# Routing of 128-token tiles to experts: row products queued behind the choice of the tile ahead, rank products at other steps, the last tile's split in a second buffer

## The chip, the cores and the metric

The kernel runs on one core of a Trainium2 chip. The metric is device time in microseconds of one launch, the median of the runs shown. Engines by the names of the profile: PE (TensorE), DVE (VectorE), ACT (ScalarE), POOL (GpSimd), SP (SyncE, which issues most DMAs). A time is better the smaller it is.

## What is computed

The reference, cut to what matters: causal attention of 2 x 12 heads (448 positions, head size 64), a dense layer with squared relu, then a layer of eight experts where each token goes to the one expert of its largest logit.

```python
scores = where(mask, -1e9, q @ k.T / sqrt(64))          # causal
x = softmax(scores) @ v                                  # -> 896 tokens x 768
h = maximum(x @ w_in, 0); x = h * h @ w_out              # 768 -> 2048 -> 768
xn = x / (norm(x) + 1e-6); en = emb / (norm(emb) + 1e-6) # 8 experts
logits = xn @ en.T / tau; idx = argmax(logits, axis=1)
gate = softmax(logits)[idx]
for e in range(8):
    m = idx == e
    out[m] = gate[m] * (maximum(x[m] @ w1[e], 0) @ w2[e]) # 768 -> 1024 -> 768
```

## The kernel before

**Precision.** Operands are split into a high half that ACT rounds (line 65) and a low half that DVE takes as the rest (line 72); three products, high by high, high by low, low by high, make one full product. So each weight piece and each block of activations costs ACT one pass and DVE one.

**Stages.** PE's instructions stand in the order in which they are written. Attention fills PE until about 180 us, the product with `w_in` until about 250. Then `b_tiles` forms y = h²·w_out for seven tiles of 128 tokens (line 639): tiles 0 and 1 together until 257.7, then tile 2, 3, 4, 5 and 6 one by one until 352.9. A tile has 16 column steps f of three pairs of matmuls (`wo<f>h`, `wo<f>l`, `wo<f>h` again). At step ends 3, 7, 11 ACT and DVE split the next part of h² into `hs`; that reuses a buffer which PE must have read. Then comes the first expert, run early with tokens known by then (`mm1`, lines 948 to 950, 352.9 to 373.3: eight blocks ft of six kc-steps of three matmuls; `mm2`, line 1036, to 392), and then all other experts, to the end.

**Routing a tile.** `route_tile(t)` is a generator. Hooks advance it by one `yield` when PE's written order comes to a given step: `CFG["rs"]` says for each tile of `b_tiles` at which step f which tile's routing goes on; `CFG["ft0"]`, `CFG["ft1"]` and `CFG["late"]` do that in the early expert, by pairs (ft, kc).
- Tiles 0 to 3 (`CFG["dve"]`): ACT squares the rows (`sq`, line 657), DVE forms eight row products with the experts' rows (`sv`, line 661; each is followed by a read of its sum). `choose` then does three Newton steps for the norm (lines 577 to 590), scales (705 to 708), takes maxima (710, 711), marks the expert (`c`, 716 and 717; the code's `c8`) and writes the one-hot `OH` (718), while ACT takes the exponentials (`ex`, 713). After a `yield` PE forms the rank products `rk` from `tri` and `OH` and from `ones` and the running sum `OHs` (721, 722); DVE and POOL finish gate and rank.
- Tiles 4 to 6: PE turns the rows (`yt`, 671), ACT and DVE split them into `yhl` (683, 72), PE forms the logits (`lgt`, 690), DVE copies them (`lgs`, 692), PE turns them back (`lg`, 696), DVE sums the two halves (`l`, 698), and then comes `choose`.

The last tile is routed during `mm1` of the early expert. `tables` follows it: `cnt` on PE (1161), `n` on DVE (1165), `z` and more, the ranks, a chain of small steps on POOL to `lane`, the one-hot `ol` on POOL (760), `rv` on DVE (753), and the table product `tabp` on PE (766), which gives the lists of tokens to all other experts. `ps_r`, tag `lg`, is one bank that `lgt`, `lg`, `rk`, `cnt` and `tabp` share in turn. `late` issues the high and low halves `mh`, `ml` of the last four weight pieces of the early expert.

**What sets the order elsewhere.** ACT's and DVE's instructions stand in the order of the scheduler: it goes by priority (`urgent` raises it) and by what is ready by its own estimate. `tc.issue_after(x)` keeps an instruction from being issued before x. An engine carries out its queue strictly in order, so an instruction that waits holds up all behind it.

Of the kernel before, what the change touches and what calls it, by code (L numbers as in the profile page):

```python
# [25 lines left out]
KC = DM // P  # L26
# [6 lines left out]
def f32(ap):  # L33
    return ap.bitcast(F32)


CFG = dict(
    first=1, hp=3000, xe=[1, 7, 8, 10, 12], turn=5, xfd=[3, 4, 5, 6], xfj=[1, 2, 3, 4],
    joint=1, mhi="A", rt6=[1, 4, 7, 9, 15], dve=(0, 1, 2, 3), neng=(),
    rs={2: [(1, 0), (2, 1)], 3: [(2, 2), (5, 0), (12, 1)], 4: [(1, 3), (7, 2)],  # L40
        5: [(2, 3), (2, 4), (3, 4), (4, 4), (5, 4), (7, 4)], 6: [(f, 5) for f in (1, 4, 7, 9, 15)]},
    rd={2: [], 3: [0, 1], 4: [2], 5: [3, 4], 6: [5]},
woh="A", h2h="A", h2l="V", et=[8, 8, 12],
    turn2=[1, 3], ft0=[(0, 3), (1, 3), (2, 3), (3, 3), (4, 3), (4, 5)], ft1=[3], ft2=[3, 5, 6, 7], late=[(2, 5), (4, 5)], ew=[2, 4, 10, 10, 10, 12], stop=0, mlo="V", xh="A", h2="A",
    wh="G", wil="G", wol="GV", warm=8, nsa=6, nwi=3, nwb=3, wo0=4, hs0=[4, 5, 8, 9], conv0=17, convs=2, pin=1,
    qsb=2, pb=2, ptb=2, qkraw=3, vraw=2, vb=2, ss=4, pts=2, pvs=2, pas=4, wsp=1,
    man=21,
# [6 lines left out]
def build(tc, qkd, vd, w_in, w_out, emb, tau, wm, cst, out, dbg_y=None):  # L54
    nc = tc.nc
    V, A, G, T, DMA = nc.vector, nc.scalar, nc.gpsimd, nc.tensor, nc.sync

    ENG = {"A": A, "V": V, "G": G, "S": DMA}
# [12 lines left out]
    def lo_of(eng, lo, x, hi):  # L71
        return eng.tensor_tensor(out=lo, in0=x, in1=hi, op=ALU.subtract)  # L72
# [19 lines left out]
    cs, at = constants()  # L92
# [13 lines left out]
    spool = tc.alloc_tile_pool(name="stage", bufs=2)  # L106
# [29 lines left out]
    last = {}  # L136
# [354 lines left out]
    for p in (ps_v, ps_t, ps_s):  # L491
# [4 lines left out]
    h2 = [h2a_pool.tile([P, NF, GT], F32, tag="h2", name="h2_0"),  # L496
          h2b_pool.tile([P, NF, GT], F32, tag="h2", name="h2_1")]
# [57 lines left out]
    bpool = tc.alloc_tile_pool(name="phb", bufs=1, reuse_waits="tile")  # L555
# [37 lines left out]
    es = rpool.tile([E, 1], F32, name="es")  # L593
# [8 lines left out]
    rows = []  # L602
# [8 lines left out]
    ent = rpool.tile([P, KC, 2 * E], F32R, name="ent")  # L611
# [39 lines left out]
    def route_tile(t, y):  # L651
        p0 = t * P
        DMA.dma_start(out=ydram[p0:p0 + P, :], in_=y)
        if t in CFG["dve"]:
            ss = rpool.tile([P, 1], F32, tag="ss", bufs=2, name="ss")
            sq = spool.tile([P, DM], BF16, tag="relu", name="sq")
            A.activation(sq, y, AF.Square, accum_out=ss)
            l = rpool.tile([P, E], F32, tag="l", bufs=2, name="l")
            for x in range(E):
                sv = spool.tile([P, DM], BF16, tag="relu", name="sv")  # L660
                V.tensor_tensor_reduce(out=sv, in0=y, in1=rows[x], scale=1.0, scalar=0.0, op0=ALU.mult, op1=ALU.add,
                                       accum_out=l[:, x:x + 1])
            yield from choose(t, ss, l)
            return
        lgt = ps_r.tile([2 * E, 2 * P], F32, tag="lg", name="lgt")
        ytt = []
        for c in range(2):
            yt = ps_h.tile([P, 512], F32, tag="h", name="yt")[:, :384].rearrange("p (a b) -> p a b", b=P)
            for j in range(3):
                kc = 3 * c + j  # L670
                T.transpose(yt[:, j], y[:, kc * P:(kc + 1) * P], ident)
            ytt.append(yt)
        ss = rpool.tile([P, 1], F32, tag="ss", bufs=2, name="ss")

# [24 lines left out]
        yield from choose(t, ss, l)
# [140 lines left out]

    NXR = (NF) * GT // (2 * DM)

    def pieces(s, res):

        for i2 in range(8):
            if i2 == 0 or (i2 == CFG["first"] and s[4] is not None):
                ereg = nc.sync.value_load((s[3] if i2 == 0 else s[4])[0:1, :], min_val=0, max_val=E - 1)
            r = state["raw"] % (NXR + 2)
            state["raw"] += 1
            if r < NXR:  # L850
                raw = mo["xraw"][:, r]
            else:
                raw = spool.tile([P, 2 * DM], F32, tag="raw", name="mraw")
            DMA.dma_start(out=raw, in_=wm[bass.ds(ereg, 1), :, 2 * i2:2 * i2 + 2, :].rearrange("o p a c -> (o p) (a c)"))
            for j in range(2):
                k = 2 * i2 + j
                pool, sl = slots[woslot[k]]
                hi = pool.tile([P, DM], F32R, tag=f"s{sl}h", name="mh")
                lo = pool.tile([P, DM], F32R, tag=f"s{sl}l", name="ml")
                x = raw[:, j * DM:(j + 1) * DM]  # L860
                copy_on(ENG[CFG["mhi"][k % len(CFG["mhi"])]], hi, x)
                lo_of(ENG[CFG["mlo"][k % len(CFG["mlo"])]], lo, x, f32(hi))
                res.append((hi, lo))
                yield

# [258 lines left out]
    for t in range(2, NTI):  # L1124
# [10 lines left out]
        if t == NTI - 1:  # L1135
# [4 lines left out]
            ew, ewl = slot_w(eslot)  # L1140
# [11 lines left out]
    y = ys[NTI - 1]  # L1152
# [283 lines left out]
```

## Time and profile before

| | |
|---|---|
| median of 3 runs | 548.42 us (547.64 to 549.15) |
| profiled execution, its own time | 548.6 us |
| its span | 546.9 us (1.7 outside it) |
| granted clock of PE, mean | 0.99 |
| PE busy | 529.6 us, 97% |
| DVE, ACT, POOL busy | 415.7, 287.6, 199.4 us |
| tile 2 of `b_tiles`, 257.70 to 274.90 | 17.20 us, PEclk 1.00 |
| tile 3, 274.90 to 296.12 | 21.22 us, PEclk 0.92 |
| tile 4, 296.12 to 312.90 | 16.78 us, PEclk 1.00 |
| early expert, 352.90 to 392.00 | 39.10 us, PE busy 37.88 |
| from 392.00 to the end | 154.90 us, PE busy 146.27 |

How to read it: the span is cut at the places where PE goes from one stage to the next. PE is busy nearly throughout; a stage of the same matmuls that lasts longer than its neighbour, or that has a granted clock under 1.00, holds a wait or its consequence. Busy time of the other engines matters only where PE waits for them. The rows on which the prediction rests have a section of their own below.

### The profile page before, as it was taken

To read this page: it belongs to the slowest core of one execution; us is meant where nothing else is said; L and a number is where in the kernel's file an instruction comes from. 1 tells how busy PE (TensorE), PEld (TensorE's weight loads), DVE (VectorE), ACT (ScalarE), POOL (GpSimd) and SP (SyncE) were. 2 spreads that over 40 slices of the span, in tenths; PEclk is the share of its full clock that TensorE was granted. 3 is DMA by queue.
4 is the path that set the end of the run, shared out by engine and by line. 5 is a ranking of instruction groups with operands and counts; after the bars stand their busy time and mean duration, and the time that the engine had idled before them with its cause. 6 is when DMAs were issued, how large, how long until landed. Compare 5 with 4: busy or idle time off the path is not lost.

```text
span 546.9 us, 9615 instructions
## 1 busy us (share of the span) xinstructions
PE 529.6 (97%) x3373; PEld 499.5 (91%) x3374; DVE 415.7 (76%) x976; ACT 287.6 (53%) x635; POOL 199.4 (36%) x273
## 2 busy tenths in 40 slices
PE   8999999999999999999989999999999999999993
PEld 5899999889999999999979989989999999999992
DVE  7888899756877968697997775886196998883641
ACT  7889887315335243434223226641386887863751
POOL 7898899916544642231010001015202302400010
PEclk9899999999999999999989999999999999999998
DMA  5667673331555555368000009402978889885310
GB/s 181 175 154 172 145 228 105 116 116 58 174 165 181 173 174 173 119 200 288 33 29 30 0 31 385 186 8 90 311 253 263 281 261 367 283 274 165 118 52 6
DMA packets 28473, 89.22 MB, mean 163 GB/s; under 512 B 2926, under 2 KB 12270, under 8 KB 28416
## 3 DMA queue, kind: packets, MB, share of 16 engines
q1 hardware_dynamic: 26880, 82.23, 47.3%
q0 software_dynamic: 1536, 6.29, 3.1%
q8 instruction: 28, 0.46, 0.3%
q14 instruction: 29, 0.24, 0.1%
HBM read 78.39 MB, written 6.32 MB: 155 GB/s over the span
## 4 chain that ended last, share of the span: by engine, by line
PE 91%; DVE 6%; ACT 1%; issue 1%; POOL 0%; POOLq 0%; DVEq 0%; ACTq 0%
PE yps L639 20%; PE ops L1036 11%; PE pa L347 7%; PE pa L349 7%; PE pa L348 7%; PE pv L323 6%; PE s L261 5%; PE pt L305 4%; PE hps L930 3%; PE ops L962 3%; PE ops L967 3%; PE hps L948 2%; PE hps L950 2%; PE hps L949 2%; PE hps L962 2%; PE hps L967 2%
## 5 line engine op out<-in xcount | busy, mean ns | idle before, releaser
L72 DVE TENSOR_TENSOR ml<-xraw,mh 128x768 fp32r<-128x768 f32 x64 | 59.5, 954 | 9.8 <-ACT mh L65 9.4
L65 ACT ACTIVATE mh<-xraw 128x768 fp32r<-128x768 f32 x64 | 52.1, 843 | 7.2 <-PE ops L962 5.8
L1036 PE MATMUL ops<-mh,act 128*128 128x384 f32 x224 | 53.5, 341 | 0.0
L323 PE MATMUL pv<-pt,v 128*128 128x448 f32 (+7 forms) x288 | 47.1, 296 | 0.6 <-ACT pt L65 0.6
L261 PE MATMUL s<-kh,q 128*128 128x128 f32 (+6 forms) x168 | 45.5, 317 | 0.7 <-ACT p L274 0.7
L274 ACT ACTIVATE p<-s,mn 128x192 f32<-128x192 f32 (+6 forms) x84 | 39.7, 476 | 11.9 <-DVE mn L271 5.2
L287 POOL TENSOR_SCALAR p<-p,rs 128x192 f32<-128x192 f32 (+6 forms) x84 | 44.1, 545 | 3.2 <-DVE rs L283 2.9
L130 DVE SCALAR_TENSOR_TENSOR w<-raw,w 128x768 int32<-128x768 int32 x32 | 42.5, 1330 | 0.7
L323 PEld LDWEIGHTS pv<-pt,v 128*128 128x128 f32 (+1 forms) x288 | 38.4, 163 | 2.7 <-ACT pt L65 1.2
L1036 PEld LDWEIGHTS ops<-mh,act 128*128 128x128 f32 x224 | 39.2, 188 | 0.8
L126 DVE TENSOR_SCALAR w<-raw 128x768 int32<-128x768 int32 x32 | 25.2, 786 | 18.5 <-POOL wi3l L72 7.2
L1062 POOL DMA_INDIRECT out<-osb,fsi x10 | 10.3, 1028 | 78.2 <-ACT osb L1057 48.8
L72 DVE TENSOR_TENSOR ml<-mraw,mh 128x768 fp32r<-128x768 f32 x32 | 30.1, 955 | 11.3 <-ACT mh L65 10.9
L729 POOL CAST gh<-g 128x1 fp32r<-128x1 f32 x7 | 1.4, 193 | 98.7 <-DVE g L727 40.1
L128 DVE SCALAR_TENSOR_TENSOR w<-raw,w 128x768 int32<-128x768 int32 x32 | 35.9, 1123 | 0.7
L271 DVE CUSTOM_DVE_ANT_0 s<-s,maskf 128x192 f32<-128x192 f32 (+6 forms) x77 | 31.8, 430 | 5.4 <-PE s L261 5.3
L353 ACT ACTIVATE relu<-pa 128x448 f32<-128x448 f32 x32 | 17.0, 538 | 34.9 <-PE pa L349 34.9
L72 DVE TENSOR_TENSOR pt<-pt 128x512 fp32r<-128x512 f32 x48 | 32.3, 682 | 3.2 <-ACT pt L65 3.1
L72 DVE TENSOR_TENSOR hs<-h,hs 128x512 fp32r<-128x512 f32 (+1 forms) x32 | 21.7, 689 | 16.7 <-ACT hs L65 16.4
L65 ACT ACTIVATE hs<-h 128x512 fp32r<-128x512 f32 (+1 forms) x32 | 17.8, 573 | 30.8 <-PE yps L639 27.6
L261 PEld LDWEIGHTS s<-kh,q 128*128 128x128 f32 x168 | 31.5, 203 | 2.4 <-ACT p L274 1.4
L65 ACT ACTIVATE pt<-pt 128x512 fp32r<-128x512 f32 x48 | 28.2, 600 | 6.1 <-PE pt L305 6.1
(471 smaller groups left out, 1683.1 us busy)
## 6 DMA issues: line engine op xcount, KB each, us to landing
xraw<-in_wm SPq DMA_DIRECT2D x32, 768.0 KB, 7.1
raw<-in_w_in SPq DMA_DIRECT2D x16, 768.0 KB, 4.2
raw<-in_w_out SPq DMA_DIRECT2D x16, 768.0 KB, 4.2
mraw<-in_wm SPq DMA_DIRECT2D x16, 768.0 KB, 5.0
qk<-in_qkd SPq DMA_DIRECT2D x11, 448.0 KB, 4.7
q<-qs SPq DMA_DIRECT2D x20, 224.0 KB, 3.8
v<-in_vd SPq DMA_DIRECT2D x12, 256.0 KB, 4.7
eb<-edram SPq DMA_DIRECT2D x8, 384.0 KB, 3.8
```

What stands on the lines that cost most here:

```text
L65: return A.activation(out, in_, AF.Copy, scale=scale)
L72: return eng.tensor_tensor(out=lo, in0=x, in1=hi, op=ALU.subtract)
L130: V.scalar_tensor_tensor(out=w[:, x], in0=raw[:, x, 0], scalar=29, in1=w[:, x], op0=ALU.logical_shift_right, op1=ALU.bitwise_or)
L261: T.matmul(ss, d["q2"][:, c, :, :, x].rearrange("p a b -> p (a b)"), d[y][:, :n], start=i_ == 0, stop=i_ == 2 and not first)
L274: last["exp", units.index(u), c] = A.activation(d["p"][c][:, :n], ss, AF.Exp, bias=mn, scale=1.0 if first else -1.0, accum_out=d["sm"][:, ...
L287: last["norm"] = G.tensor_scalar(out=p, in0=p, scalar1=rs[:, COL[c]:COL[c] + 1], scalar2=1.0, op0=ALU.mult, op1=ALU.mult)
L323: T.matmul(d["pv"][:, j * P:S] if h else d["pv"][0:D, j * P:S], d[x][:, j, 1:3].rearrange("p a b -> p (a b)") if h else d[x][:, j, 0], pt[ ...
L347: T.matmul(ps, wh[:, c], xhi[:, kc, gs], start=(kc == 0), stop=False)
L348: T.matmul(ps, wh[:, c], xlo[:, kc, gs], start=False, stop=False)
L349: T.matmul(ps, wl[:, c], xhi[:, kc, gs], start=False, stop=(kc == KC - 1))
L639: T.matmul(ps[t][c][:, :384], x, w[:, c * 384:(c + 1) * 384], start=(f == 0 and w is wh and x is hi), stop=(f == NF - 1 and x is lo))
L1036: T.matmul(ps[c], x, ww[:, col[c]], start=(fc == 0 and x is hh and ww is wh), stop=(fc == 7 and x is hl))
```

## The change

For tiles 0 to 3 the row products are now written inside `issue_after` on the `OH` of the tile ahead (from tile 1 on). Three rank products stand at earlier steps: `rk(0)` at step 2 of tile 3 (was 5), `rk(1)` at step 10 (was 12), `rk(2)` at step 5 of tile 4 (was 7). In the last tile the second `yhl` has a buffer of its own (tag `ysb`, two buffers) and both halves are split one behind the other, with the six `lgt` products in a row at (1,2); `lg` moves from (3,3) to (2,0), `rk` from (4,3) to (3,3), `cnt` from (4,5) to (4,1). The last four weight pieces are issued at (2,1) and (4,2) instead of (2,5) and (4,5), and their low halves on DVE are held behind `OH` of the last tile (first two) and behind `n` (last two).

```diff
-    rs={2: [(1, 0), (2, 1)], 3: [(2, 2), (5, 0), (12, 1)], 4: [(1, 3), (7, 2)],
+    rs={2: [(1, 0), (2, 1)], 3: [(2, 2), (2, 0), (10, 1)], 4: [(1, 3), (5, 2)],
...
-    turn2=[1, 3], ft0=[(0, 3), (1, 3), (2, 3), (3, 3), (4, 3), (4, 5)], ft1=[3], ft2=[3, 5, 6, 7], late=[(2, 5), (4, 5)], ew=[2, 4, 10, 10, 10, 12], stop=0, mlo="V", xh="A", h2="A",
+    turn2=[1, 3], ft0=[(0, 3), (1, 2), (2, 0), (3, 3), (4, 1)], ft1=[3], ft2=[3, 5, 6, 7], late=[(2, 1), (4, 2)], ew=[2, 4, 10, 10, 10, 12], stop=0, xh="A", h2="A",
...
-            for x in range(E):
+            with tc.issue_after(last["oh"].ins) if t else nullcontext():
+                for x in range(E):
...
+        due = []
         for c in range(2):
-            yhl = bpool.tile([P, 3, 2, P], F32R, tag="yhl", name="yhl")
+            again = t == NTI - 1 and c == 1
+            yhl = bpool.tile([P, 3, 2, P], F32R, name="yhl", **(dict(tag="ysb", bufs=2) if again else dict(tag="yhl")))
             last["yh"] = A.copy(yhl[:, :, 0], ytt[c])
             last["yl"] = lo_of(V, yhl[:, :, 1], ytt[c], f32(yhl[:, :, 0]))
+            due.append((c, yhl))
             if t == NTI - 1 and c == 0:
                 square()
+                continue
             yield
-            for j in range(3):
-                kc = 3 * c + j
+            for d, x in due:
+                for j in range(3):
+                    kc = 3 * d + j
...
-                lo_of(ENG[CFG["mlo"][k % len(CFG["mlo"])]], lo, x, f32(hi))
+                with ExitStack() as es:
+                    for at in pin:
+                        es.enter_context(tc.issue_after(at))
+                    lo_of(V, lo, x, f32(hi))
...
     def late():
-        while True:
+        for at in ("oh", "n"):
+            pin.append(last[at].ins)
...
+            pin.clear()
```

DVE around `OH` of tile 0. Before, the products that stand between the steps of the choice are tile 2's; all eight of tile 1 stand further ahead, between the Newton steps (`ISA` is a row product or the read of its sum):

```order
L717 TENSOR_REDUCE m<-c_3156 128x1
L589 TENSOR_TENSOR ynr<-ynr,ynt 128x1
L661 ISA sv,l<-ysb,eb 128x768
L661 ISA l 128x1
L661 ISA sv,l<-ysb,eb 128x768
L661 ISA l 128x1
L726 TENSOR_SCALAR g<-m 128x1
L718 TENSOR_SCALAR OH<-ct,m 128x8
```

And the same place in the changed kernel:

```order
L724 TENSOR_REDUCE m<-c_3156 128x1
L589 TENSOR_TENSOR ynr<-ynr,ynt 128x1
L733 TENSOR_SCALAR g<-m 128x1
L725 TENSOR_SCALAR OH<-ct,m 128x8
L662 ISA sv,l<-ysb,eb 128x768
L662 ISA l 128x1
L662 ISA sv,l<-ysb,eb 128x768
L662 ISA l 128x1
```

Tile 1's products moved from ahead of `OH` of tile 0 to behind it, and tile 2's from there to behind `OH` of tile 1.

PE in tile 3, at step 2, as a piece of the difference (the rank products of tile 0, with their weight loads):

```order
 L639 MATMUL yps<-wo1l,hs 128x384 x2
 L639 MATMUL yps<-wo1h,hs 128x384 x2
+L728 LDWEIGHTS tri
+L728 MATMUL rk<-OH,tri 128x8
+L729 LDWEIGHTS ones
+L729 MATMUL rk<-OHs,ones 128x8
 L639 MATMUL yps<-wo2h,hs 128x384 x2
 L639 MATMUL yps<-wo2l,hs 128x384 x2
```

They moved here from three steps later, between `wo4h` and `wo5h`.

DVE in the last tile, from the end of the logits to the choice, before (`ml` are low halves of weight pieces, `act` the early expert's own results):

```order
L692 COPY lgs<-lgt 16x256
L72 TENSOR_TENSOR ml<-xraw,mh 128x768 x2
L954 SCALAR_TENSOR_TENSOR act<-hps,act 128x2x128 x2
L698 TENSOR_REDUCE l<-lg 128x8
L954 SCALAR_TENSOR_TENSOR act<-hps,act 128x2x128
L708 TENSOR_SCALAR l<-l,sc 128x8
```

And in the changed kernel, from the choice's end to the ranks:

```order
L725 TENSOR_SCALAR OH<-ct,m 128x8
L72 TENSOR_TENSOR ml<-xraw,mh 128x768 x2
L734 RECIPROCAL g<-g 128x1
L730 TENSOR_TENSOR OHs<-OHs,OH 128x8
L1180 TENSOR_TENSOR tw<-OH,me_4378 128x56
L966 SCALAR_TENSOR_TENSOR act<-hps,act 128x2x128
L740 TENSOR_TENSOR c_4304<-rk,OH 128x8
L1182 TENSOR_REDUCE tm<-tw 128x7
L966 SCALAR_TENSOR_TENSOR act<-hps,act 128x2x128
L741 TENSOR_REDUCE ranks<-c_4304 128x1
L1177 TENSOR_TENSOR n<-cnt,me_4378 128x8
L72 TENSOR_TENSOR ml<-xraw,mh 128x768 x2
```

The four `ml`, two of which stood ahead of `lgs` and two behind it, now stand two behind `OH` and two behind `n`, ahead of the ranks and `z`.

## Rows read from the trace of the kernel before

**Rows 1.** the page: chain that ended last, by engine; a group, busy us and mean ns
```profile
PE 91%; DVE 6%; ACT 1%; issue 1%; POOL 0%; POOLq 0%; DVEq 0%; ACTq 0%
...
L72 DVE TENSOR_TENSOR ml<-xraw,mh 128x768 fp32r<-128x768 f32 x64 | 59.5, 954 | 9.8 <-ACT mh L65 9.4
```

**Rows 2.** PE's waits, whole span: waiting line, releaser, us in total, times, longest
```profile
PE rk L721 <- DVE OH L718: 2.5, 1, 2.5
```

**Rows 3.** stretches: length; busy us of PE, PEld, DVE, ACT, POOL; PEclk, DMA, GB/s
```profile
274.90:296.12 21.22, 18.72 (x101) 18.24 (x101) 18.06 (x92) 5.38 (x15) 2.89 (x9) 0.92 0.05 20
296.12:312.90 16.78, 16.78 (x99) 16.62 (x99) 13.09 (x46) 4.62 (x10) 0.51 (x3) 1.00 0.06 23
284.00:285.00 1.00, 1.00 (x5) 1.00 (x5) 1.00 (x7) 0.00 (x0) 0.19 (x1) 0.50 0.00 0
```

**Rows 4.** PE's timeline, tile 3: start us, us, instruction, [idle before and releaser]
```profile
279.13 0.51 PE L639 MATMUL yps<-wo4h,hs 128*128 128x384 f32 x2
...
279.82 0.51 PE L639 MATMUL yps<-wo4h,hs 128*128 128x384 f32 x2
282.83 0.19 PE L721 MATMUL rk<-OH,tri 128*128 128x8 bf16 x1 [2.50 <-DVE OH L718]
...
282.91 0.99 PE L639 MATMUL yps<-wo5h,hs 128*128 128x384 f32 x2
...
286.25 0.52 PE L639 MATMUL yps<-wo6h,hs 128*128 128x384 f32 x2
```

**Rows 5.** DVE's timeline in tiles 2 and 3
```profile
266.90 0.14 DVE L588 TENSOR_SCALAR ynt<-ynt 128x1 f32<-128x1 f32 x1
...
278.49 0.22 DVE L716 SCALAR_TENSOR_TENSOR c<-l,m,ct 128x8 f32<-128x8 f32 x1
...
279.99 0.69 DVE L72 TENSOR_TENSOR hs<-h,hs 128x512 fp32r<-128x512 f32 x1 [1.22 <-ACT hs L65]
...
280.74 0.95 DVE L661 CUSTOM_DVE_ANT_0 sv<-ysb,eb 128x768 bf16<-128x768 f32 x1
```

**Rows 6.** ACT's timeline in tiles 2 and 3
```profile
270.86 0.73 ACT L65 ACTIVATE hs<-h 128x256 fp32r<-128x256 f32 x2 [3.25 <-PE yps L639]
...
279.33 0.63 ACT L65 ACTIVATE hs<-h 128x512 fp32r<-128x512 f32 x1 [1.07 <-PE yps L639]
```

**Rows 7.** PE's timeline in the early expert: last tile's products, then the table
```profile
361.95 0.29 PE L696 MATMUL lg<-ident,lgs 16*128 16x16 f32 x2
...
364.23 0.28 PE L950 MATMUL hps<-act,ml 128*128 128x256 f32 x1
365.70 0.18 PE L721 MATMUL rk<-OH,tri 128*128 128x8 bf16 x1 [1.19 <-DVE g L727]
...
366.56 0.18 PE L1161 MATMUL cnt<-OHs,ones 128*128 128x8 bf16 x1
...
376.39 0.88 PE L766 MATMUL tabp<-rv,ol 128*128 128x108 f32 x7
```

**Rows 8.** timelines of ACT, DVE, POOL around the last tile's choice and table
```profile
354.70 0.46 ACT L683 CAST yhl<-yt 128x384 fp32r<-128x384 f32 x1
...
357.52 0.48 ACT L683 CAST yhl<-yt 128x384 fp32r<-128x384 f32 x1 [1.01 <-PE lgt L690]
357.89 3.05 ACT L65 ACTIVATE mh<-xraw 128x768 fp32r<-128x768 f32 x4
...
363.38 0.17 DVE L698 TENSOR_REDUCE l<-lg 128x8 f32<-128x32 f32 x1
...
365.42 0.22 DVE L718 TENSOR_SCALAR OH<-ct,m 128x8 bf16<-128x8 f32 x1
...
366.79 0.17 DVE L1165 TENSOR_TENSOR n<-cnt,me 128x8 f32<-128x8 f32 x1 [0.28 <-PE cnt L1161]
...
375.11 0.93 DVE L753 TENSOR_TENSOR rv<-oc,vals 128x756 fp32r<-128x756 f32 x1
...
370.65 4.58 POOL L760 TENSOR_SCALAR ol<-ct,lane 128x128 fp32r<-128x128 f32 x7
```

More of the change, by code (lines that the diff above doesn't have):

```diff
@@ L658, in route_tile @@
             l = rpool.tile([P, E], F32, tag="l", bufs=2, name="l")
-            for x in range(E):
-                sv = spool.tile([P, DM], BF16, tag="relu", name="sv")
-                V.tensor_tensor_reduce(out=sv, in0=y, in1=rows[x], scale=1.0, scalar=0.0, op0=ALU.mult, op1=ALU.add,
-                                       accum_out=l[:, x:x + 1])
+            with tc.issue_after(last["oh"].ins) if t else nullcontext():
+                for x in range(E):
+                    sv = spool.tile([P, DM], BF16, tag="relu", name="sv")
+                    V.tensor_tensor_reduce(out=sv, in0=y, in1=rows[x], scale=1.0, scalar=0.0, op0=ALU.mult,
+                                           op1=ALU.add, accum_out=l[:, x:x + 1])
             yield from choose(t, ss, l)
@@ L680, in route_tile @@
             square()
+        due = []
         for c in range(2):
-            yhl = bpool.tile([P, 3, 2, P], F32R, tag="yhl", name="yhl")
+            again = t == NTI - 1 and c == 1
+            yhl = bpool.tile([P, 3, 2, P], F32R, name="yhl", **(dict(tag="ysb", bufs=2) if again else dict(tag="yhl")))
             last["yh"] = A.copy(yhl[:, :, 0], ytt[c])
             last["yl"] = lo_of(V, yhl[:, :, 1], ytt[c], f32(yhl[:, :, 0]))
+            due.append((c, yhl))
             if t == NTI - 1 and c == 0:
                 square()
+                continue
             yield
-            for j in range(3):
-                kc = 3 * c + j
-                T.matmul(lgt, ent[:, kc], yhl[:, j].rearrange("p a b -> p (a b)"), start=(kc == 0), stop=(kc == KC - 1))
+            for d, x in due:
+                for j in range(3):
+                    kc = 3 * d + j
+                    T.matmul(lgt, ent[:, kc], x[:, j].rearrange("p a b -> p (a b)"), start=(kc == 0), stop=(kc == KC - 1))
+            due = []
         lgs = spool.tile([2 * E, 2, P], F32, tag="relu", name="lgs")
@@ L841, in build @@
     NXR = (NF) * GT // (2 * DM)
+    pin = []
     def pieces(s, res):
@@ L1164, in tables @@
         V.tensor_scalar(out=me1, in0=ear["e1"], scalar1=ear["m"], scalar2=None, op0=ALU.mult)
-        V.tensor_tensor(out=n, in0=cnt, in1=me1, op=ALU.subtract)
+        last["n"] = V.tensor_tensor(out=n, in0=cnt, in1=me1, op=ALU.subtract)
         tw = small([NTI, E], "tw")
```

## The prediction, made blind

> **What bounds the kernel now.** I read the page first: the chain that ended last is 91% TensorE (PE), so the time is PE's instruction stream plus the places where that stream stands still [rows 1]. Next comes the view of PE's waits. Only two of its eight lines lie in the code that the diff touches, and both are the rank product `rk` waiting for a tile's choice: once for 2.5 us [rows 2], once for 1.2 us, which stands behind the instruction itself in the timeline [rows 7]. Then the table by stage says what the first costs beyond the wait itself. Tile 3 of `b_tiles` takes 21.22 us at a mean granted clock of 0.92; tile 4, with the same matmuls, takes 16.78 us at 1.00. One microsecond picked from behind the wait shows 0.50, the lower of the two levels [rows 3]. The timelines of PE, VectorE (DVE) and ScalarE (ACT) then give the dates. All dates below are on the axis of the profiled execution of before, 548.6 us with 1.7 of them outside its span (the table above); it is 0.2 above the median of the three runs, 548.42.
>
> **Place 1: tile 3 of b_tiles.** PE's column steps take 16.78/16 = 1.05 us each [rows 3]. In steps of 0.345 (279.13 to 279.82 is two of them) the pair after the one at 279.82 was due at 280.17; in fact `rk` issues at 282.83, so 2.66 us are lost. The next five pairs run from 282.91 to 286.25, 3.34 us instead of 5 x 0.347 = 1.73, so another 1.61 goes to the half clock [rows 4]. Together **4.27 us**, which agrees with the 21.22 - 16.78 = 4.44 of the stage table, where tile 3 also holds one more pair of rank products.
>
> Why it waits: `rk(0)` needs the one-hot OH of tile 0. Tile 0's row products were done at 266.90, yet its c starts only at 278.49, because products of tiles 1 and 2, up to 0.95 each, stand between its small steps, and one more after 280.74 [rows 5]. The change puts tile 1's products behind OH of tile 0 and tile 2's behind OH of tile 1. Now:
>
> - *rk(0), now at column step 2.* From 266.90 on DVE has only tile 0's small steps and one split `hs` that it takes after ACT's, which ends at 270.86 + 0.73 = 271.6 [rows 5, 6]. With that split (under 0.8) and the few steps behind it (c to OH, under 1), OH(0) comes at about 273.0 to 273.4. PE reaches step 2 at 274.90 + 2 x 1.05 = 277.0 [rows 3]. Nearly 4 us of cover, so all 4.27 should go.
> - *rk(1), now at step 10 (was 12).* This is the tight one. With no stall PE starts step 4 at 279.13 [rows 4], plus 0.13 for the two rank products ahead, hence step 8 at 279.26 + 4 x 1.05 = 283.46 and step 10 at 285.56. By DVE's own work OH(1) would come near 284.3: eight products of at most 0.95 from 273.1, two splits of about 0.7, and some 2.4 for the choice (2.04 from `l` to OH in the last tile, 363.38 to 365.42, plus the last Newton steps) [rows 5, 8]. But the order puts a split of `hs` ahead of the last steps, and that is released by PE at step 8. In before the same release took 0.20 to ACT's start and 0.66 from there to DVE's (279.13, 279.33, 279.99), and 0.69 on DVE [rows 4 to 6]. So 283.46 + 0.20 + 0.66 + 0.69 = 285.01, then three small steps at 0.07 and OH itself, 0.22: 285.44. The margin is 0.1 us. I take 0, with a wait of up to 0.5 in the range.
> - *rk(2), tile 4, step 5 (was 7).* OH(2) at the latest 285.44 + 8 x 0.95 + 2 x 0.69 + 2.4 = 296.8; PE reaches step 5 of tile 4 at 274.90 + 0.13 + 21 x 1.05 + 0.1 = 297.2. Cost 0, thin. rk(3), in tile 5, stays where it is and has some 3 us.
>
> The products are not lengthened, only queued later; POOL's and SP's order is unchanged. What is late next is the choice of tiles 1 and 2, and that is in the margins above. Term: **-4.27**.
>
> **Place 2: the last tile, in the early expert.** Matmuls issue every 0.117 here. `rk(6)` was due at 364.23 + 0.12 = 364.35 and issues at 365.70 with a wait for DVE of 1.19: 1.35 to 1.38 lost [rows 7]. The clock does not drop afterwards: from 365.70 to `cnt` at 366.56 there are six matmuls and the ranks, 6 x 0.117 + 0.1 and little more [rows 7].
>
> - *What moves on PE.* Both halves' six `lgt` products stand in a row at step (1,2), `lg` goes from (3,3) to (2,0), that is nine kc-steps of 0.35 earlier, `rk` from (4,3) to (3,3), 2.1 us earlier, `cnt` from (4,5) to (4,1). The number of matmuls is the same, so PE's own cost is 0.
> - *The second buffer for the split.* It lets ACT and DVE split the second half at once instead of after `lgt` of the first. Its former reader is the store of tile 5, issued a whole tile before: 0.
> - *The choice.* PE reaches `lg` at 361.95 - 3.15 = 358.8 [rows 7]. From the reduction `l` to OH it took 363.38 to 365.42, 2.04 us, with two of the experts' products and a wait among it [rows 8]. So OH(6) comes at 361.2 to 361.4, and PE reaches `rk` at 364.35 - 2.1 = 362.3. The wait goes: **-1.38**. The cover is 0.9 us. It would be used up if ACT were late with the first two `act`: four pieces' `mh`, 3.05 together [rows 8], now stand ahead of them, but they start some 2.4 earlier, since the second split's cast, which waited for `lgt` until 357.52, can follow the first one's end at 355.1; so they end near 358.5.
> - *cnt.* It takes the bank of `rk`, which DVE must have read, and two low halves `ml` (0.95 each [rows 1]) now stand behind OH and ahead of that read. DVE gets there about 0.1 later than PE: **+0.11**.
> - *tabp, the table product.* PE reached it at 376.39; now at 376.39 - 1.38 + 0.11 = 375.12 [rows 7]. Its inputs: `n` came 0.23 after `cnt` (366.56, 366.79) and `rv` ended at 375.11 + 0.93 = 376.04, that is 9.25 after `n` [rows 7, 8]. In the changed order `n` starts at about 364.4 (`cnt` at 363.85, the 0.23, and one `act` in between), two `ml` behind it take 1.74, and then the 9.25: 375.4. The ranks for POOL pass behind the same `ml`, at about 366.4 as before, so `ol` ends near 370.65 + 4.58 = 375.23 as before [rows 8]. So a small new wait, 375.4 - 375.12: **+0.28**. Bounds: 0 if DVE's chain runs with less idle time, 1.27 if `rv` ends as late as before.
>
> The experts that follow load by this table. It comes about 0.7 earlier and PE about 1.0, and none of the other lines of PE's waits stands behind the early expert, so I take 0.
>
> **Sum.** -4.27 - 1.38 + 0.11 + 0.28 = -5.26; 548.6 - 5.26 = **543.3**, 0.2 less against the median.
>
> **A rule against it.** The rows show that the 2.50 us wait in tile 3 was followed by about 3.3 us at 0.50, while the 1.19 us wait in the early expert was followed by none [rows 3, 4, 7]. The Trainium skill, "TensorE: Matmul & The Clock Gate", section "Part 1: The HAM clock gate (the "warmup" mystery)", says that the throttled state is the default and that activity releases it. By that, a new wait of PE may bring the half clock with it. For a wait of 0.5 at `rk(1)` the sum by the row of place 2 would be -5.26 + 0.5 = -4.76; by the rule it would be that plus the 1.61 of tile 3, -3.15, which is rival (b). The rows show one case of each, so I give the rule a small chance.
>
> **Rivals.**
> (a) *The table takes back what the last tile gives.* `rv` ends as before, at 376.04, since DVE's chain is fed by POOL and the `ml` only change places. Then `tabp` issues at 376.4 as before and only place 1 remains: 548.6 - 4.27 = 544.3. For it: POOL's `ol` really has no reason to be earlier. Against: `ol` ends 0.8 before `rv` [rows 8]. Chance 0.16.
> (b) *rk(1) waits and the clock falls.* A margin of 0.1 rests on four small latencies. If OH(1) is 0.5 late and the half clock comes as it did in tile 3, 0.5 + 1.61 return: 545.4. For it: the split is tied to PE itself, so PE cannot outrun it nor be outrun. Against: the shorter wait of place 2 brought no half clock. Chance 0.09.
> (c) *Slower: the queue of products becomes the bound.* Tile 1's eight products can no longer start while DVE waits for tile 0's choice. If a split that waits on PE at the end of tile 2 stood ahead of OH(0), the eight products (up to 7.6) would all begin some 4 us later, and OH(1) with them. Each microsecond goes to PE, plus 1.61 for the clock. The point from which it decides is 5.26 - 1.61 = 3.65 late; at 5.5 late the time is 548.6 + 1.85 = 550.5. For it: 1.1 us of slack of DVE is all there is. Against: in the order the only split ahead of OH(0) is the one that ACT delivers at 271.6 [rows 6]. Chance 0.03.
> (d) *The change does not do what it says:* the waits move to other instructions of the same steps, and the time stays at 548 to 549. Against: no other work stands between tile 0's products and its choice now. Chance 0.05.
>
> **How the numbers follow.** My forecast has 0.67, (a) 0.16, (b) 0.09, (c) 0.03, (d) 0.05. Predicted: 543.3. The forecast's own bounds: `tabp` 0 instead of 0.28 and the stray of single runs give 542.5; the `rk(1)` wait of 0.5 and `tabp` at 0.8 give 544.3. (a) lies at its end; (b) reaches 545.4, of which I take most: 542.5 to 545.2. A measurement of this kernel can tell 0.3%, 1.65 us, from no change; so faster means below 546.8. Faster: forecast, (a) and (b), 0.92; same 0.05; slower 0.03.
>
> **What would show it.** Right: no wait at `rk` in tile 3, the clock of its stage at 1.00 and its length near 16.9; OH(0) near 273; `rk(6)` without a wait; at `tabp` a wait of 0 to 0.5. Wrong: half clock anywhere in tiles 3 to 5 (then b), a wait at `tabp` of 1 us or more (a), a DVE idle for a split just ahead of OH(0) or OH(1) (c). It would also be wrong if the experts' first weights after 392, or the tail, became late with PE 5 us ahead; the trace of before shows no wait of PE there, so I give that nothing beyond the range.

## The result and the profile after

The changed kernel takes 543.53 us, median of 4 runs (543.11 to 544.05), the kernel before 548.03 (4 runs, 547.57 to 549.15): a ratio of 0.9915, interval 0.9896 to 0.9935. The prediction was 543.3, the range 542.5 to 545.2. The profiled execution took 543.2 us, its span 541.5.

PE's waits, the whole list of the changed kernel (waiting line, releaser, us in total, times, longest), no longer have `rk` in them; what is left is attention's, and two at `wp` and `enp`:

```profile
PE wp L392 <- DVE wz L154: 1.4, 1, 1.4
PE pt L305 <- DVE pt L72: 0.8, 1, 0.8
PE s L261 <- POOL kl L72: 0.7, 2, 0.5
PE s L261 <- ACT p L274: 0.7, 1, 0.7
PE pt L305 <- POOL p L287: 0.6, 2, 0.4
PE pv L323 <- ACT pt L65: 0.6, 1, 0.6
PE enp L610 <- DVE em L599: 0.2, 1, 0.2
```

The table by stage, for tiles 3 and 4 of `b_tiles` and for `mm1` and `mm2` of the early expert (stretch and length; busy us of PE, PEld, DVE, ACT, POOL; PEclk, DMA share, GB/s):

```profile
274.40:291.48 17.08, 17.08 (x102) 16.76 (x101) 16.12 (x62) 4.59 (x11) 4.08 (x6) 1.00 0.06 24
291.48:308.31 16.83, 16.83 (x99) 16.67 (x99) 15.30 (x61) 4.50 (x10) 2.33 (x3) 1.00 0.06 23
348.34:367.33 18.99, 18.96 (x162) 18.36 (x162) 17.00 (x69) 8.48 (x19) 5.58 (x23) 1.00 0.06 22
367.33:386.51 19.18, 19.07 (x118) 18.41 (x116) 6.89 (x25) 2.72 (x6) 8.82 (x10) 1.00 0.63 212
```

The same table of the kernel before for the early expert (its tiles 3 and 4 stand in [rows 3]):

```profile
352.94:373.27 20.33, 19.11 (x163) 18.37 (x162) 17.84 (x69) 8.46 (x19) 6.97 (x25) 1.00 0.05 21
373.27:392.08 18.81, 18.81 (x118) 18.45 (x117) 6.81 (x25) 2.72 (x6) 7.12 (x8) 1.00 0.65 216
```

So in the two profiled executions:

| stage | before | after | difference |
|---|---|---|---|
| start to tile 2 | 257.72 | 257.22 | -0.50 |
| tile 2 | 17.18 | 17.18 | 0 |
| tile 3 | 21.22 | 17.08 | -4.14 |
| tiles 4 to 6 | 56.82 | 56.86 | +0.04 |
| `mm1` of the early expert | 20.33 | 18.99 | -1.34 |
| `mm2` of the early expert | 18.81 | 19.18 | +0.37 |
| the rest of the span | 154.82 | 154.99 | +0.17 |
| sum | 546.90 | 541.50 | -5.40 |

The first line is the same code in both kernels. Among the profiled executions of this study tile 2 began at anything from 256.73 to 258.91, so one execution's total carries some 2 us that the change has no part in. That is why the experiments below are read by stages, and totals only where there were several runs.

DVE's timeline of the changed kernel shows the three choices, and ahead of the second one a split that waited for ACT:

```profile
272.37 0.22 DVE L725 TENSOR_SCALAR OH<-ct,m 128x8 bf16<-128x8 f32 x1
...
283.83 0.69 DVE L72 TENSOR_TENSOR hs<-h,hs 128x512 fp32r<-128x512 f32 x1 [0.96 <-ACT hs L65]
...
284.63 0.23 DVE L725 TENSOR_SCALAR OH<-ct,m 128x8 bf16<-128x8 f32 x1
...
295.38 0.23 DVE L725 TENSOR_SCALAR OH<-ct,m 128x8 bf16<-128x8 f32 x1
```

PE's timeline shows the rank products that need them; none has a wait:

```profile
276.52 0.18 PE L728 MATMUL rk<-OH,tri 128*128 128x8 bf16 x1
...
285.08 0.18 PE L728 MATMUL rk<-OH,tri 128*128 128x8 bf16 x1
...
296.69 0.18 PE L728 MATMUL rk<-OH,tri 128*128 128x8 bf16 x1
```

`OH` of tile 0 ends at 272.37 + 0.22 = 272.59, 3.9 us ahead of PE, where before PE waited 2.5 us for it [rows 4]. `OH` of tile 1 ends at 284.63 + 0.23 = 284.86, 0.22 ahead of PE, and the split of 0.69 just before the choice's end (0.96 idle, released by ACT) is the one that the prediction named. `OH` of tile 2 is 1.1 ahead.

In the early expert, PE's timeline:

```profile
357.70 0.18 PE L728 MATMUL rk<-OH,tri 128*128 128x8 bf16 x1
...
359.27 0.18 PE L1173 MATMUL cnt<-OHs,ones 128*128 128x8 bf16 x1
...
370.74 0.96 PE L773 MATMUL tabp<-rv,ol 128*128 128x108 f32 x7
```

and DVE's around it:

```profile
356.54 0.22 DVE L725 TENSOR_SCALAR OH<-ct,m 128x8 bf16<-128x8 f32 x1
...
359.00 0.15 DVE L740 TENSOR_TENSOR c<-rk,OH 128x8 f32<-128x8 f32 x1
...
369.65 0.94 DVE L760 TENSOR_TENSOR rv<-oc,vals 128x756 fp32r<-128x756 f32 x1
```

`rk` of the last tile issues 9.36 us after the stage's start (357.70 - 348.34), before it was 12.76 (365.70 - 352.94, [rows 7]); of these 3.40, 2.1 are the step that it was moved and 1.3 the wait that is gone. `cnt` issues right after the read of `rk`'s bank (`c` at 359.00 + 0.15); `tabp` issues 3.41 after `mm2` began, before 3.12, right behind `rv`, which ends at 369.65 + 0.94 = 370.59.

### The profile page after: what moved, and what is told of

Same layout as the page of the kernel before. It is cut to its first block, busy times and chain, and to the rows that moved or that the text cites. A ratio compares the mean times of both kernels' runs of the same rounds, so it can differ in the third digit from the quotient of the medians.

```text
span 541.5 us, 9616 instructions
## 1 busy us (share of the span) xinstructions
PE 527.2 (97%) x3374; PEld 496.2 (92%) x3374; DVE 413.5 (76%) x976; ACT 287.4 (53%) x635; POOL 205.6 (38%) x273
## 4 chain that ended last, share of the span: by engine, by line
PE 73%; DVE 14%; DMA 6%; issue 2%; ACT 2%; POOL 2%; SPq 0%; POOLq 0%; DVEq 0%; ACTq 0%
PE yps L639 16%; PE ops L1048 11%; PE pv L323 7%; PE s L261 5%; PE pt L305 4%; DVE w L128 4%; DVE w L130 3%; PE hps L942 3%; PE ops L974 3%; PE ops L979 3%; DMA raw<-in_w_in 2%; PE pa L347 2%; PE pa L348 2%; PE pa L349 2%; DVE w L126 2%
## 5 line engine op out<-in xcount | busy, mean ns | idle before, releaser
L287 POOL TENSOR_SCALAR p<-p,rs 128x192 f32<-128x192 f32 (+6 forms) x84 | 45.5, 564 | 2.6 <-DVE rs L283 2.3
L261 PE MATMUL s<-kh,q 128*128 128x128 f32 (+6 forms) x168 | 44.0, 308 | 0.7 <-ACT p L274 0.7
L130 DVE SCALAR_TENSOR_TENSOR w<-raw,w 128x768 int32<-128x768 int32 x32 | 42.5, 1331 | 0.7
L128 DVE SCALAR_TENSOR_TENSOR w<-raw,w 128x768 int32<-128x768 int32 x32 | 37.0, 1160 | 0.7
L736 POOL CAST gh<-g 128x1 fp32r<-128x1 f32 x7 | 3.5, 505 | 88.1 <-DVE OHs L730 32.3
L126 DVE TENSOR_SCALAR w<-raw 128x768 int32<-128x768 int32 x32 | 22.9, 715 | 17.4 <-POOL wi3l L72 7.3
```

The lines of the kernel that those rows point to most:

```text
L126: V.tensor_scalar(out=w[:, x], in0=raw[:, x, 1], scalar1=3, scalar2=0x3FFFFFFF, op0=ALU.logical_shift_left, op1=ALU.bitwise_and)
L128: V.scalar_tensor_tensor(out=w[:, x], in0=raw[:, x, 1], scalar=-0x40000000, in1=w[:, x], op0=ALU.bitwise_and, op1=ALU.bitwise_or)
L130: V.scalar_tensor_tensor(out=w[:, x], in0=raw[:, x, 0], scalar=29, in1=w[:, x], op0=ALU.logical_shift_right, op1=ALU.bitwise_or)
L261: T.matmul(ss, d["q2"][:, c, :, :, x].rearrange("p a b -> p (a b)"), d[y][:, :n], start=i_ == 0, stop=i_ == 2 and not first)
L287: last["norm"] = G.tensor_scalar(out=p, in0=p, scalar1=rs[:, COL[c]:COL[c] + 1], scalar2=1.0, op0=ALU.mult, op1=ALU.mult)
```

## The experiments

### Each place alone

`place1_only` has the first place of the change and the last tile of before; `place2_only` the reverse.

`place1_only`:

```diff
-            again = t == NTI - 1 and c == 1
+            again = False
...
-                continue
...
-ft0=[(0, 3), (1, 2), (2, 0), (3, 3), (4, 1)], late=[(2, 1), (4, 2)]
+ft0=[(0, 3), (1, 3), (2, 3), (3, 3), (4, 3), (4, 5)], late=[(2, 5), (4, 5)]
...
-            pin.append(last[at].ins)
+            pass
```

`place2_only`:

```diff
-            with tc.issue_after(last["oh"].ins) if t else nullcontext():
+            with nullcontext():
...
-    3: [(2, 2), (2, 0), (10, 1)], 4: [(1, 3), (5, 2)],
+    3: [(2, 2), (5, 0), (12, 1)], 4: [(1, 3), (7, 2)],
```

> The row products behind the choice of the tile ahead and the earlier rank products, with the last tile as in the kernel before. Theory (the two places are separate, place 1 carries most): tile 3 of b_tiles takes 17.1 us at clock 1.00 instead of 21.22, no wait at rk there; in the early expert the wait at rk of 1.2 stays and mm1 takes 20.3; time 548.0 - 4.1 = 543.9. Rival (the table takes back all that the last tile gives, so place 2 is worth nothing): the same time as the whole change, 543.5. Rival (place 1 works only together with place 2): 546 or more.

> The new last tile alone; row products and steps of the rank products as in the kernel before. Theory: tile 3 stays at 21.2 with its wait of 2.5 at half clock behind it; mm1 of the early expert 19.0 instead of 20.33, from there to the next expert 19.2 instead of 18.8; net -1.0, time 547.0. Rival (the table takes it all back): 548.0, with mm2 of the early expert longer by 1.3.

Measured: `place1_only` 543.99 us against 547.82 of before in the same session (ratio 0.992, interval 0.9894 to 0.9945); tile 3 takes 17.08. `place2_only` 547.0 (0.9983, 0.9967 to 0.9998); its early expert takes 18.99 and 19.15. The places are separate: -3.8 and -0.8. The rival by which the table takes back the whole of place 2 falls, though the interval of `place2_only` ends close to 1.

The stage table and PE's timeline of `place2_only` show more. Its tile 3 has the routing of the kernel before, and the wait at the first `rk` is the same 2.50, but in this execution the clock stays at 1.00, where I had expected the half clock and a tile 3 of 21.2:

```profile
274.84:295.48 20.64, 17.47 (x102) 16.92 (x101) 18.06 (x92) 5.26 (x15) 2.87 (x9) 1.00 0.05 20
```

```profile
282.78 0.18 PE L728 MATMUL rk<-OH,tri 128*128 128x8 bf16 x1 [2.50 <-DVE OH L725]
...
282.84 0.60 PE L639 MATMUL yps<-wo5h,hs 128*128 128x384 f32 x2
283.27 0.52 PE L639 MATMUL yps<-wo5l,hs 128*128 128x384 f32 x2
...
284.00 0.52 PE L639 MATMUL yps<-wo6h,hs 128*128 128x384 f32 x2
...
291.18 0.17 PE L728 MATMUL rk<-OH,tri 128*128 128x8 bf16 x1 [0.67 <-DVE ynr L589]
```

The pairs behind the wait come every 0.36 us, not every 0.65 as in [rows 4]. Instead PE reaches `rk` of tile 1 early enough to wait there too, 0.67 us. (The releaser `ynr` is the step of DVE that stands right behind `OH`.) The kernel before, in the timelines of DVE and PE, has no wait there:

```profile
290.96 0.22 DVE L718 TENSOR_SCALAR OH<-ct,m 128x8 bf16<-128x8 f32 x1
```

```profile
291.82 0.18 PE L721 MATMUL rk<-OH,tri 128*128 128x8 bf16 x1
```

`OH` of tile 1 ends 16.28 us after the tile's start there (290.96 + 0.22 - 274.90) and 16.29 in `place2_only`, so PE can't pass that place sooner, whatever its clock. The stage of `place2_only` takes 20.64. So place 1 is worth 20.64 - 17.08 = 3.56 us where the clock holds, and 4.14 where it falls: the half clock of before had hidden a second wait.

### Queue or steps

`old_steps` is the whole change with the rank products at the steps of before; `steps_only` is the whole change with the products free on DVE; `ranks_later` leaves the products free and puts the rank products later than before.

`old_steps`:

```diff
-    3: [(2, 2), (2, 0), (10, 1)], 4: [(1, 3), (5, 2)],
+    3: [(2, 2), (5, 0), (12, 1)], 4: [(1, 3), (7, 2)],
```

`steps_only`:

```diff
-            with tc.issue_after(last["oh"].ins) if t else nullcontext():
+            with nullcontext():
```

`ranks_later` has that too, and:

```diff
-    3: [(2, 2), (2, 0), (10, 1)], 4: [(1, 3), (5, 2)],
+    3: [(2, 2), (8, 0)], 4: [(0, 1), (1, 3), (7, 2)],
...
-    rd={2: [], 3: [0, 1], 4: [2], 5: [3, 4], 6: [5]},
+    rd={2: [], 3: [0], 4: [1, 2], 5: [3, 4], 6: [5]},
```

> The whole change, but the rank products of tiles 0 to 2 at the steps of before (5 and 12 in tile 3, 7 in tile 4). Theory (only the date of OH matters, a rank product that comes later costs PE nothing): tile 3 17.1, no wait, time as the whole change, 543.5. Rival (the earlier steps carry a part, since the reads of rk and the ranks behind them would delay DVE's products of the next tile): a wait of 0.5 to 1.5 at rk of a later tile, time 544 to 545.

> The whole change without the order of the row products: they are free to stand ahead of the choice of the tile ahead, while rk(0) stands at step 2. Theory (the queue of DVE is the cause): OH(0) comes at about 281 to 282.5 as before, PE reaches rk(0) at 276.5 and waits 4 to 6 us, with half clock behind it: tile 3 takes 23 to 25 us, time 549 to 551. Rival (the steps of the rank products carry the gain): tile 3 17.1, time 543.5.

> The new last tile, DVE's row products free as before, and the rank products of tiles 0 and 1 later instead of earlier: step 8 of tile 3 and step 0 of tile 4 (of before: 5 and 12 in tile 3). Theory (PE loses only where it comes to a rank product ahead of the choice, and nothing else needs the rank early): OH(0) at 282.8 and OH(1) near 291 of the kernel before are then early enough, no wait in tiles 3 and 4, tile 3 17.1, time as the whole change, 543.5. Rival (the choices are late on DVE anyway, and the wait moves on to the next rank product, of tile 1 or 2): a wait of 0.5 to 2 in tile 4, time 544 to 546.

Measured: `old_steps` 543.36 us (0.9906, 0.988 to 0.9932), tile 3 17.05, no wait at a rank product. The earlier steps are worth nothing; the queue alone does it, and the old steps leave more margin.

`steps_only` 548.36 (1.0002, 0.9985 to 1.0019), though its last tile is the new one. PE's waits, and the stage table of its tile 3:

```profile
PE rk L728 <- DVE OH L725: 3.0, 1, 3.0
PE rk L728 <- DVE ynr L589: 1.0, 1, 1.0
```

```profile
275.86:297.27 21.41, 17.38 (x102) 16.83 (x102) 18.15 (x92) 5.38 (x15) 2.90 (x9) 1.00 0.05 20
```

Two waits, of 3.0 and 1.0, and tile 3 takes 21.41. I had expected 23 to 25, from a wait of 4 to 6 and the half clock. The wait was shorter because `OH` of tile 0 came earlier: in DVE's timeline one row product and no split stand between `c` and `OH`, where before it was the split and two products. And the clock stayed at 1.00 behind a wait longer than the one of before. The rival, that the steps carry the gain, falls.

`ranks_later` 549.57 (1.0017, 1.0002 to 1.0032): here my theory failed and the rival held. Tiles 3 and 4 in the stage table, and PE's timeline at `rk` of tile 2:

```profile
274.67:291.65 16.98, 16.98 (x102) 16.66 (x101) 15.38 (x71) 4.64 (x12) 1.58 (x3) 1.00 0.06 24
291.65:315.42 23.77, 19.40 (x101) 19.17 (x101) 14.89 (x67) 5.02 (x14) 3.62 (x9) 0.86 0.05 17
```

```profile
303.56 0.17 PE L728 MATMUL rk<-OH,tri 128*128 128x8 bf16 x1 [4.37 <-DVE ynr L589]
...
304.40 0.84 PE L639 MATMUL yps<-wo7l,hs 128*128 128x384 f32 x2
305.04 0.84 PE L639 MATMUL yps<-wo7h,hs 128*128 128x384 f32 x2
```

The wait has left tile 3 (16.98) and stands in tile 4, 4.37 long, with the half clock behind it: 23.77 instead of 16.83. Of these 6.94 us 4.37 are the wait and some 2.5 the half clock. DVE's timeline shows what stands ahead of this choice, the first of eight row products and the choice itself:

```profile
293.60 0.95 DVE L662 CUSTOM_DVE_ANT_0 sv<-ysb,eb 128x768 bf16<-128x768 f32 x1
...
303.29 0.22 DVE L725 TENSOR_SCALAR OH<-ct,m 128x8 bf16<-128x8 f32 x1
```

The eight are tile 3's, from 293.60 to 301.75, and they stand ahead of `OH` of tile 2, which ends at 303.51. In the kernel before they began at 297.80, behind that `OH` (294.39). So it is the pattern of place 1 one tile later: with PE's wait in tile 3 gone, the next tile's products have come ahead of the choice. Why the scheduler put them there is not shown. Moving the reader later only hands the delay on; the order on DVE removes it.

### The margin at rk of tile 1

`rk1_f9` moves the product of tile 1 one step earlier, `rk1_f8` two, to (8, 1):

```diff
-    3: [(2, 2), (2, 0), (10, 1)], 4: [(1, 3), (5, 2)],
+    3: [(2, 2), (2, 0), (9, 1)], 4: [(1, 3), (5, 2)],
```

> The whole change with the rank product of tile 1 one column step earlier, at 9. In the whole change PE reached it at 285.08 and OH was ready at 284.86, a margin of 0.2. Theory: PE arrives 1.05 earlier and waits about 0.85, tile 3 takes 17.9 instead of 17.08, nothing of it comes back later: 544.4. Rival (the split that PE releases at step 8 and that stands ahead of the choice moves with PE, so the margin is kept): no wait, 543.5. If the half clock comes, 1.5 more.

> The same at step 8. Theory: PE waits about 1.9, tile 3 takes 19.0, time 545.4, or 1.5 more with half clock. Rival: no wait, 543.5.

The rank product and the stage of `rk1_f9`, from PE's timeline and the stage table:

```profile
286.59 0.17 PE L728 MATMUL rk<-OH,tri 128*128 128x8 bf16 x1 [0.73 <-DVE OH L725]
```

```profile
276.08:294.00 17.92, 17.19 (x101) 16.80 (x101) 16.96 (x64) 4.59 (x11) 4.08 (x6) 1.00 0.06 23
```

and of `rk1_f8`:

```profile
285.16 0.17 PE L728 MATMUL rk<-OH,tri 128*128 128x8 bf16 x1 [1.78 <-DVE OH L725]
```

```profile
274.66:293.62 18.96, 17.18 (x102) 16.79 (x102) 17.95 (x68) 4.59 (x11) 4.08 (x6) 1.00 0.06 22
```

17.92 and 18.96: 0.84 and 1.88 more than 17.08, as the margin of 0.2 says for one and two steps of 1.05. Nothing came back later; the totals of one execution each were 545.55, of which 1.7 more than in the changed kernel had gone by before tile 2, and 545.13. The split ahead of the choice didn't keep the margin: it depends on step 8, not on where `rk` stands. The clock stayed at 1.00 behind 0.73 and behind 1.78.

### What removes the wait of the last tile

`ml_pins_only` has place 1 and, of the last tile, only the low halves behind the choice; `ml_free` is the whole change without that.

`ml_pins_only` is `place1_only` with `pin.append` kept and another `late` (against the changed kernel; `place1_only` has `[(2, 5), (4, 5)]`):

```diff
-late=[(2, 1), (4, 2)]
+late=[(3, 4), (5, 0)]
```

`ml_free` is the changed kernel with

```diff
-            pin.append(last[at].ins)
+            pass
```

> Place 1 as in the whole change; in the last tile only the low halves of the last four pieces are moved behind its choice, two behind OH and two behind n; the shared buffer of the split, the steps of lgt, lg, rk and cnt are as before. Theory (the wait at rk came from the two low halves, 1.8 us, that stood between lgs and l on DVE): OH comes 1.2 earlier, the wait at rk falls from 1.35 to 0 to 0.2, mm1 19.0 to 19.2; but cnt stands two kc-steps later than in the whole change, so rv is later and the table product waits 1.0 to 1.3, mm2 20.0. Time near 543.9. Rival (the buffer and the earlier lg are what remove the wait): the wait at rk stays at 1.0 or more, mm1 20.0 or more.

> The whole change, but the low halves of the last four pieces are not held behind the choice; the order then puts them among the Newton steps of the last tile. Theory: 3.5 us of DVE ahead of the choice, OH at some 12 us after the early expert's start instead of 8.2, a wait at rk of 2 to 3 us, mm1 21 to 22 (more with half clock); no wait at the table product, mm2 18.8; time 545 to 547. Rival (the buffer and the steps alone give the gain): mm1 19.0 to 19.3.

PE's waits and the early expert of `ml_pins_only`:

```profile
PE tabp L772 <- DVE rv L759: 1.4, 1, 1.4
PE cnt L1172 <- DVE c L739: 0.8, 1, 0.8
```

```profile
347.84:367.87 20.03, 19.19 (x163) 18.54 (x162) 16.23 (x63) 8.34 (x19) 6.38 (x21) 1.00 0.06 21
367.87:388.31 20.44, 19.06 (x117) 18.41 (x116) 8.09 (x31) 2.71 (x6) 10.07 (x12) 1.00 0.62 212
```

The wait at `rk` is gone without the second buffer and without earlier steps, as the theory said. But `cnt` waits 0.8 for DVE's read of `rk`'s bank, which I hadn't counted, and `tabp` waits 1.4: `mm1` gains 0.30 and `mm2` loses 1.63. The time of one execution, 545.02, is above `place1_only`. The four pieces, with their high halves on ACT, are also issued later here than in `place1_only`; this run alone doesn't separate that from the order of the low halves on DVE.

PE's wait and `mm1` of `ml_free`:

```profile
PE rk L728 <- DVE g L734: 2.3, 1, 2.3
```

```profile
348.32:370.08 21.76, 19.20 (x162) 18.38 (x162) 18.35 (x73) 8.48 (x19) 8.47 (x27) 1.00 0.05 20
```

With the buffer and the earlier steps but the low halves ahead of the choice, `rk` waits 2.3 and `mm1` takes 21.76, more than before the change; `mm2` is 18.83. One execution, 545.55. So buffer and steps without the order leave a wait, and the order of the low halves decides over it. That the buffer and the earlier steps are what keeps the table from giving the gain back follows from `ml_pins_only` beside the changed kernel; no run tells buffer, steps and the earlier issue of the pieces apart.

### The new wait at the table product

`ml_behind_rv` and `ml_behind_lists` put the low halves of the last two pieces behind `rv` or behind `fsi`, the last of the token lists made from the table, instead of behind `n`. `two_early` splits two pieces ahead of the last tile's own split and two behind `OH`.

The main lines of the edit of `ml_behind_rv`, which also has `late=[(2, 1)]`; `ml_behind_lists` is the same with "fsi", and `two_early` has no second pair left to issue there:

```diff
-        for at in ("oh", "n"):
+        for at in ("oh", "rv"):
...
+            if i == 1:
+                hooks.setdefault(3, []).append(wl_late)
             mm2([(eslot, i - 1)], ew, hooks)
```

> The whole change, but the low halves of the last two weight pieces stand behind rv instead of behind n. Theory (the small new wait at the table product comes from these two, 1.74 us of DVE ahead of the ranks and of z): rv and ol end some 1.7 us earlier, no wait at the table product, mm2 of the early expert 18.8 instead of 19.18, mm1 unchanged at 19.0; time 543.1 to 543.5, 0.3 to 0.4 less than the whole change. Rival (the wait there is POOL's ol, which has its own reason): mm2 stays at 19.2.

> The whole change, but two of the last four pieces are split ahead of the last tile's own split and the other two behind OH; none behind n. Theory: the table product does not wait, mm2 18.8, but the split of the last tile comes up to 0.7 late for lgt, mm1 19.0 to 19.7; time 543.2 to 544. Rival (POOL's ol sets the table product): mm2 stays at 19.2.

> The whole change, but the low halves of the last two pieces stand behind fsi, the last of the token lists made from the table product, so that neither the table nor the lists wait for them; piece 14 is then ready some 1 us before PE needs it. Theory (what went wrong with these two behind rv is that the token gather and the weight loads met): the table product does not wait, the gather is issued 1 us earlier against PE than in the whole change and lands in time, mm2 18.8, time 543.1. Rival (any earlier start of the weight loads against the gather slows the gather down): PE waits 1 to 2.5 for the gathered tokens again, mm2 20 to 23, time 544 to 545.

`ml_behind_rv`: 544.72 us (0.9934, 0.9915 to 0.9954). `tabp` issues 3.12 after `mm2`'s start, with no wait, so the two low halves were its cause; that part of the theory holds. But PE then waits for gathered tokens, and `mm2` takes 22.76 with the half clock behind the wait. The trace is of the slowest of five executions, 547.38, and the other four took 544.02 to 545.11, so the usual cost is probably smaller. PE's timeline and the stage table:

```profile
382.73 0.83 PE L1096 MATMUL xt<-ident,xr 128*128 128x128 f32 x3 [2.18 <-DMA xr<-ydram,fgi]
```

```profile
368.16:390.92 22.76, 20.58 (x117) 19.97 (x116) 7.37 (x23) 2.72 (x6) 8.75 (x8) 0.93 0.71 251
```

POOL's timeline has the gather's issue, here of `ml_behind_rv` and then of the changed kernel:

```profile
374.19 1.16 POOL L1086 DMA_INDIRECT xr<-ydram,fgi  x1 [2.46 <-issue]
```

```profile
373.51 1.16 POOL L1086 DMA_INDIRECT xr<-ydram,fgi  x1 [2.54 <-issue]
```

Against the start of `mm2` the gather was issued at 6.03 us, in the changed kernel at 6.18, so it was not late; it landed late. Its two transfers landed 8.1 to 8.4 us after their issue; in the changed kernel they landed after 4.2 to 4.9, and PE used them without a wait. In the same stretch SP issues the loads of the next weights (`mraw`): 1.3 us behind the gather here, 3.3 behind it in the changed kernel. That the two met is my reading; no run here changed only that.

`two_early`: one execution, 545.55; `mm2` 18.81, but `mm1` 20.67, with waits of 0.7 behind the late split and 0.4 at `cnt`, and a delay of 0.2 at `rk`, whose `OH` ended just ahead of it. It loses more than it gains.

`ml_behind_lists`: 542.89 us (0.9911, 0.9891 to 0.993). Its early expert:

```profile
347.87:366.87 19.00, 18.96 (x163) 18.37 (x162) 16.62 (x72) 8.48 (x19) 7.27 (x25) 1.00 0.06 22
366.87:385.67 18.80, 18.80 (x117) 18.44 (x116) 7.57 (x23) 2.72 (x6) 7.83 (x8) 1.00 0.73 263
```

`mm2` is back at 18.80, PE waits neither for the table nor for the tokens, and the rival falls in the form that says that PE would wait again. The gather did land later than in the changed kernel, after 5.9 to 6.6 us, with the loads 1.9 us behind it; it was issued 0.9 earlier against the start of `mm2`. The kernel keeps the 0.38 that the change gave back. By its median it is the fastest kernel here, but the totals can't tell 0.4 us from the changed kernel; the stage table does.

## Why the prediction was right, and where it was not

**Place 1, the mechanism: right.** `OH` of tile 0 was expected at 273.0 to 273.4 and ended at 273.1 on the axis of before (272.59 and the 0.50 by which the front differs). `OH` of tile 1 was expected to end at 285.44, 0.1 ahead of PE; it ended 0.22 ahead, behind the split that was named. `OH` of tile 2 was 1.1 ahead, expected 0.4 or more. `steps_only`, `old_steps` and `ranks_later` show that the order on DVE is the cause. One reading was short: from 280.74 on DVE had two products ahead of `OH` of tile 0, not "one more", and the idle time and the split at 279.99 [rows 5] were part of the delay too; the sum doesn't use either.

**Place 1, the size: right for the profiled execution, too large where the clock holds.** The term was -4.27, the stage gave -4.14. The step at fault is "another 1.61 goes to the half clock": it was taken as a part of the stall that belongs to it. `place2_only` shows the same wait without it, and then a second wait of 0.67 at `rk` of tile 1 in its place. There the gain is 3.56, from one execution. With place 2's 0.97 that makes 4.53, and the medians differ by 548.03 - 543.53 = 4.50. Against the medians the -5.26 of the sum was 0.76 too much. That the median still came out 0.2 from the forecast is partly luck: the sum was taken off an execution 0.6 above this median of before.

**Place 2: the size right, the cause in part.** `rk` -1.38 and `cnt` +0.11 make -1.27; `mm1` gave -1.34. `tabp` +0.28; it issued 0.29 later in `mm2`, and `mm2` as a whole lost 0.37. The chain that was followed there, from `cnt` by way of the two low halves to `rv`, is confirmed by `ml_behind_rv` and `ml_behind_lists`, where the wait goes with them. The text gave the choice's earlier date to the second buffer and the earlier `lg`; `ml_free` has both and its `rk` waits 2.3, while `ml_pins_only` has neither and its `rk` doesn't wait: the order of the low halves, which the text counted only as a cost at `cnt` and `tabp`, is what takes the wait away, and the buffer and the steps pay for the table.

**The rivals.** (a) falls by `place2_only` and by `mm2`: 0.37 came back, not 1.27. (b) did not happen; `rk1_f9` and `rk1_f8` give its price without the clock, 0.84 and 1.88. (c) did not happen: `OH` of tiles 0 and 1 was in time. (d) falls for this kernel; `ranks_later` shows what it would look like, a wait of 4.37 that has moved to the next tile. "PE shows no wait from there on, so I take 0" was right for this change, but thinner than it looked: in `ml_behind_rv` the gather missed its date.

## What to carry to other kernels

When short dependent steps that another engine waits for share an in-order queue with long independent work, put the long work behind the result by order, and only then move the reader; moving the reader alone carries the wait to the next place. Before a wait is priced, look at what it hides: another wait further on, an order of the next tile's work that may change with it, and a clock that may or may not fall. Work that is pushed behind a result lands in front of the next one, so follow the chain to its last reader, here the token lists and the gather.

## What the runs showed of the hardware

The half clock behind a wait of PE can't be read off the wait's length. It came behind 2.50 us in the profiled execution of before [rows 3, 4], behind 4.37 in `ranks_later` and behind 2.18 in `ml_behind_rv`; it did not come behind 2.50 in `place2_only`, behind 3.02 in `steps_only`, behind 2.3 in `ml_free`, nor behind 1.78 and 0.73 in the kernels with `rk` moved. Each of these is one execution. The mean granted clock is known for every execution, those without a trace too, and fits that: it is 0.993 or less in 26 of 46 executions of before, in 6 of 10 each of `place2_only` and `steps_only`, in 10 of 10 of `ranks_later`, and in 1 of 16 of the changed kernel, `place1_only`, `old_steps` and `ml_behind_lists` together, none of which waits at `rk` in tiles 3 and 4. Such a mean doesn't say where in the span the clock fell. So an estimate should carry the half clock as a chance, not as a term. The Trainium skill, "TensorE: Matmul & The Clock Gate", section "Part 1: The HAM clock gate (the "warmup" mystery)", says that the gate's observation is not reset when a kernel starts and that the effect varies from run to run. The traces agree with the second (2.50 with it and 2.50 without it at the same instruction); no run here shows the first.

A gather from device memory that landed 4.2 to 4.9 us after its issue in the changed kernel took 5.9 to 6.6 in `ml_behind_lists` and 8.1 to 8.4 in `ml_behind_rv`; the next weight loads were issued 3.3, 1.9 and 1.3 us behind it. Three executions in that order don't show the cause. How little the gather had to spare stands in no list of waits.
